# Rebuilding the first step of a fused recurrence and feed-forward kernel: order of the loads, scalings and transposes

## The chip, the core and the metric

The kernel runs on one core of one Trainium2 chip. The metric is the device time of one execution in microseconds; lower is better. Three runs of the kernel before gave 597.99, 598.65 and 599.09 us, median 598.65.

## The reference

Two blocks in a row, in float32. The first is a recurrence over time, for 4 batches and 8 heads of 48 channels, 768 tokens each; the second is a feed-forward block on the 3072 tokens.

```python
for t in range(S):
    kt, vt, rt, wt = (k[:, :, t], v[:, :, t], r[:, :, t], w[:, :, t])
    cur = np.einsum('bhd,bhe->bhde', u[None] * kt, vt)
    y[:, :, t] = np.einsum('bhd,bhde->bhe', rt, state + cur)
    state = wt[:, :, :, None] * state + np.einsum('bhd,bhe->bhde', kt, vt)
...
x = y.transpose(0, 2, 1, 3).reshape(B * S, H * D)      # 3072 x 384
h = x @ w_in                                           # 384 x 2048
g = h * erf(softplus(h))
out = g @ w_out                                        # 2048 x 384
```

The two weight matrices are given in double precision and are turned into float32 on the chip, from pairs of 32-bit words.

## The kernel before, in words

**Steps.** The work is cut into 12 steps. A step takes one chunk of 128 tokens of two of the four batches, with all heads: 16 pairs of batch and head. Steps alternate between the two pairs of batches; steps 0 and 1 have no state before them. In the document "step one" or "the first step" is `s == 0`, "step two" is `s == 1`.

**Recurrence.** Inside a step the decays are handled by a ladder of six levels (`attend`, L625). At level n blocks of 2^(n-1) tokens are joined. `level_products` (L444) issues 64 small matmuls, the products of R with K. `scale` (L257, the instruction is L263) then multiplies half of R and half of K, in place in the tile `in`, by the products of decays of their blocks, which `prepare` (L267) made on GpSimd (L315, tile `tot_sb`). `take_level` (L460) copies what belongs to this level from PSUM into `own`, with a mask on VectorE (L464) up to level five and by ScalarE copies (L471) at level six. Level one uses a copy `rk1` of R and K with the bonus u multiplied into half of it: in the first step VectorE does that for R (L284, L288) and ScalarE for K (L292, L295), for one batch at a time. The matmuls of a level wait for the scaling of the level before, and the scaling waits until the matmuls have read their operands.

**After the ladder.** `from_own` (L477, matmul L486) adds what is inside the chunk to `y` in PSUM, for one half of the heads at a time. K is transposed by TensorE (L680) and copied to `kT` by ScalarE (L684). `state_part` (L531, matmul L538) makes the change of the state for both halves of the chunk. The state after the first half goes to `middle` (L712), is faded on GpSimd (L713) and added to the second part for the next state (L715). `through_state` (L500) adds the state's share to `y` (L512), copies `y` to `y3` and `xT` (L519 to L522), and sends six small transfers (L526) that fill up the rows of `xT` from `y3`: three from SP's queue, three from ScalarE's.

**Feed-forward.** `hidden` (L744) multiplies `w_in_sb` with `xT` (L777) and copies to `h` (L786), in eight pieces per step; `project` and `project_fast` multiply with `w_out_sb`. The feed-forward of a step runs between the levels of the steps after it: `beside` (L925) issues a piece behind each level, so the first pieces (L777) come in step two and need `xT` of step one and the weight pairs one after another.

**Weights.** `convert` (L185) is a generator that is sent letters. Each pair of weight rows is loaded ("l", L199), scaled on ScalarE ("s": the high words into a PSUM tile `pp1`, L212, the low words to `rest`, L214), shifted on VectorE ("h", L220), joined with its sign on VectorE (L228) and with the low part on GpSimd (L232; "o"). "j" stands for "ho". The table `CONVERT` says which letters are sent at which place of which of the first four steps; place n stands behind level n+1.

**Order.** All instructions of an engine run in the order in which the program issues them; SP's queue of transfers too. Transfers use eight semaphores in turn, so a transfer also waits until the one eight before it has landed. PSUM has two tiles of two banks for products (`pp0`, `pp1`), two banks for `m` and two for `y`. `keep_busy` (L635), `stay_warm` (L643) and the 20 matmuls at L1026 compute nothing that is used; they keep TensorE busy.

Of the kernel before, what the change touches and what calls it, by code (L numbers as in the profile page):

```python
# [61 lines left out]
def kernel(  # L62
# [81 lines left out]
    def load_w(s, parts=1):  # L144
        ws[s] = ins.tile([P, JP, C], FP32, name="w")
        n = JP // parts
        for i in range(parts):
            nc.sync.dma_start(
                out=ws[s][:, i * n : (i + 1) * n], in_=rkw[s][:, 2, i * n : (i + 1) * n]
            )  # L150

    def load_step(s, parts=1):
        t = ins.tile([P, 2, JP, C], FP32, name="in")
        vt = ins.tile([P, NH, D], FP32, name="v")
        n = JP // parts
        for i in range(parts):
            nc.sync.dma_start(
                out=t[:, :, i * n : (i + 1) * n], in_=rkw[s][:, 0:2, i * n : (i + 1) * n]
            )
        if s <= DIRECT:  # L160
            load_w(s, parts)
        if not s:
            nc.sync.dma_start(out=mask_sb[:], in_=masks)
        elif s == 2:
            nc.sync.dma_start(out=block_sb[:], in_=block_mask)
            nc.sync.dma_start(out=u_row[:], in_=u_rows)
# [18 lines left out]
    def convert(weights):  # L185
# [5 lines left out]
        def load(i):  # L191
# [3 lines left out]
            if src.dtype == FP32:  # L195
# [3 lines left out]
            nc.sync.dma_start(  # L199
                out=words[:].rearrange("p i n two -> p i (n two)"), in_=src.bitcast(I32)  # L200
            )
            held[i] = [words]

        def scale(i):
            if i in held:
                words = held[i][0]
                low, high = words[:, :, :, 0], words[:, :, :, 1]
                base = ps_p.tile([P, 2, NP * C], FP32, name="pp1")[:, :, :DM]
                rest = wide.tile([P, 2, DM], I32, name="rest", bufs=2)


                nc.scalar.mul(out=base, in_=high.bitcast(FP32), mul=2.0**-112)  # L212

                nc.scalar.mul(out=rest[:], in_=low.bitcast(U32), mul=2.0**-29)  # L214
                held[i] += [base.bitcast(I32), rest]

        def shift(i):
            if i in held:
                bits = held[i][1]
                nc.vector.tensor_scalar(  # L220
                    out=bits, in0=bits, scalar1=3, scalar2=None, op0=ALU.logical_shift_left
                )

        def join(i):
            if i in held:
                words, bits, rest = held.pop(i)
                into = weights[i][0].bitcast(I32)
                nc.vector.scalar_tensor_tensor(  # L228
                    out=into, in0=words[:, :, :, 1], scalar=-(1 << 31), in1=bits,
                    op0=ALU.bitwise_and, op1=ALU.bitwise_or,  # L230
                )
                nc.gpsimd.tensor_tensor(out=into, in0=into, in1=rest[:], op=ALU.add)  # L232

        stages = {"l": load, "s": scale, "h": shift, "o": join}
        done = dict.fromkeys(stages, 0)
        for _ in range(3):
            load(done["l"])
            done["l"] += 1
        while True:
            what = yield  # L240
            for stage in {"j": "ho"}.get(what, what):
                stages[stage](done[stage])
                done[stage] += 1
            if weights[0][1].dtype != FP32:
                turns["converting"] = 0 < done["s"] and done["o"] < len(weights)
                turns["next"] = 0
# [10 lines left out]
    def scale(s, level):  # L257

        in_t, tots = loaded[s][0], ready[s][1]
        half, nb = 1 << (level - 1), JP * C >> level  # L260
        n = 1 if s > DIRECT and level == LOG else 2
# [238 lines left out]
    def through_state(s, xT):  # L500
# [19 lines left out]
        for j in range(NJ):  # L520
            nc.scalar.copy(xT[:, 0:2, j * C : (j + 1) * C], y[:, 0, j])
        nc.scalar.copy(xT[:, 2, :].rearrange("p (j t) -> p j t", j=NJ), y[:, 1, :, 0])  # L522
        for kk in range(KT):
            n = D // KT
            for e, queue in enumerate((nc.sync, nc.sync if s > DIRECT else nc.scalar)):
# [5 lines left out]
    def state_part(s, kT, ps):  # L531

        vt = loaded[s][1]
        for n in range(JP):
            for h in range(1 if s >= n_steps - SPC else NC):
                for e in range(NE):
                    t = slice(h * HC, (h + 1) * HC)
                    nc.tensor.matmul(  # L538
                        ps[h][rows(e), n, :D],
# [32 lines left out]
    def attend_late(s, run):  # L572
# [38 lines left out]
        ps = [ps[:, h] for h in range(NC)]  # L611
# [587 lines left out]
```

## Time and profile before

| | us |
|---|---|
| median of three runs | 598.65 |
| the profiled execution | 598.5 |
| its span | 596.3 |
| TensorE busy in the span | 584.7 |
| VectorE, ScalarE, GpSimd busy | 440.1, 361.8, 274.5 |
| first matmul of the feed-forward (L777) starts at | 34.40 |
| TensorE busy from 75 to 596 | 517.3 of 521 |
| DMA traffic in the span | 63.33 MB, of it 18.05 MB in the first 80 us |

Times of instructions count from the start of the span. A row of the timeline has the start, the busy time, the engine, the line of the kernel, the operation, the tile written and the tiles read, the shapes, how many were merged, and in brackets how long the engine was idle before it and what ended that. PE is TensorE, DVE VectorE, ACT ScalarE, POOL GpSimd, SP the engine whose queue issues most transfers; a name with a q is the engine's own queue. A float32 matmul appears as two passes, each with a load of weights (PEld) and a matmul.

### The profile page before, as it was taken

To read this page: it belongs to the slowest core of one execution; us is meant where nothing else is said; L and a number is where in the kernel's file an instruction comes from. 1 tells how busy PE (TensorE), PEld (TensorE's weight loads), DVE (VectorE), ACT (ScalarE), POOL (GpSimd) and SP (SyncE) were. 2 spreads that over 40 slices of the span, in tenths; PEclk is the share of its full clock that TensorE was granted. 3 is DMA by queue.
4 is the path that set the end of the run, shared out by engine and by line. 5 is a ranking of instruction groups with operands and counts; after the bars stand their busy time and mean duration, and the time that the engine had idled before them with its cause. 6 is when DMAs were issued, how large, how long until landed. Compare 5 with 4: busy or idle time off the path is not lost.

```text
span 596.3 us, 16645 instructions
## 1 busy us (share of the span) xinstructions
PE 584.7 (98%) x7290; PEld 501.7 (84%) x7290; DVE 440.1 (74%) x516; ACT 361.8 (61%) x473; POOL 274.5 (46%) x296
## 2 busy tenths in 40 slices
PE   8889999999999999999999999999999999999997
PEld 7667788678758758898898898898898898898997
DVE  5688598799996799799799799799799525023140
ACT  2547788717534398765765666666666664746710
POOL 4348365610588549749449449449459000000000
PEclk9999999999999999999999999999999999999999
DMA  8377381541315324334334335334331300000000
GB/s 320 124 278 234 118 290 58 217 141 20 134 38 159 66 95 168 71 108 169 72 107 168 73 106 169 73 107 134 71 107 54 71 9 26 2 21 13 2 27 26
DMA packets 51376, 63.33 MB, mean 106 GB/s; under 512 B 34920, under 2 KB 40296, under 8 KB 49896
## 3 DMA queue, kind: packets, MB, share of 16 engines
q1 hardware_dynamic: 50824, 62.03, 32.3%
q8 instruction: 57, 0.93, 0.6%
q10 hardware_dynamic: 480, 0.25, 0.2%
q14 instruction: 15, 0.12, 0.1%
HBM read 52.39 MB, written 8.69 MB: 102 GB/s over the span
## 4 chain that ended last, share of the span: by engine, by line
PE 88%; DVE 6%; issue 2%; ACT 2%; DMA 1%; POOL 1%; SPq 0%; DVEq 0%; ACTq 0%; POOLq 0%
PE m L777 40%; PE m L885 28%; PE m L809 8%; PE pp L452 6%; PE y L486 2%; DVE in L263 2%; PE pp L538 1%; PE y L512 1%; DMA in<-in_rkw 1%; PE pp L680 1%; DVE sums L367 1%; DVE words L381 1%; DVE own L464 1%; ACT rk L292 1%; DVE w_in_sb L228 0%
## 5 line engine op out<-in xcount | busy, mean ns | idle before, releaser
L777 PE MATMUL m<-xT,w_in_sb 128*128 128x256 f32 x1152 | 257.3, 382 | 2.3 <-DVE w_in_sb L228 1.3
L777 PEld LDWEIGHTS m<-xT,w_in_sb 128*128 128x128 f32 x1152 | 216.0, 190 | 34.5 <-issue 3.7
L786 ACT COPY h<-m 128x512 f32<-128x512 f32 x96 | 55.6, 580 | 84.2 <-PE m L777 84.1
L263 DVE TENSOR_TENSOR in<-in,tot_sb 128x1024 f32<-128x1024 f32 (+1 forms) x60 | 78.3, 1305 | 24.9 <-PE pp L452 23.8
L377 POOL TENSOR_TENSOR rk<-words 128x528 f32<-128x528 f32 (+3 forms) x28 | 41.6, 1485 | 91.4 <-DVE sums L367 81.0
L381 POOL TENSOR_TENSOR words<-words,rest 128x528 f32<-128x528 f32 (+10 forms) x77 | 79.1, 1027 | 6.0
L809 PE MATMUL m<-w_out_sb,h 128*128 128x384 f32 x192 | 64.3, 491 | 0.0
L809 PEld LDWEIGHTS m<-w_out_sb,h 128*128 128x128 f32 x192 | 35.7, 190 | 23.6
L885 PE MATMUL m<-mixed,h 128*128 128x192 f32 x288 | 51.1, 331 | 0.0
L885 PE MATMUL m<-w_out_sb,h 128*128 128x192 f32 x288 | 50.3, 329 | 0.0
L733 ACT ACT_TABLE_LOAD x36 | 46.2, 1283 | 2.4 <-issue 1.7
L885 PEld LDWEIGHTS m<-w_out_sb,h 128*128 128x128 f32 x288 | 46.9, 190 | 0.5
L885 PEld LDWEIGHTS m<-mixed,h 128*128 128x128 f32 x288 | 46.6, 190 | 0.9
L737 ACT ACT_TABLE_LOAD x36 | 46.2, 1283 | 1.7 <-DVE room L868 1.1
L452 PEld LDWEIGHTS pp<-in 48*64 48x64 f32 (+1 forms) x2368 | 34.0, 125 | 14.8 <-issue 8.1
L885 PE MATMUL m<-w_out_sb,room 128*128 128x192 f32 x256 | 44.2, 326 | 0.0
L452 PE MATMUL pp<-in 48*64 48x64 f32 (+1 forms) x2368 | 38.7, 212 | 4.0 <-issue 1.8
L315 POOL TENSOR_TENSOR tot_sb<-tot_sb 128x256 f32<-128x256 f32 (+4 forms) x60 | 40.4, 674 | 4.5
L885 PEld LDWEIGHTS m<-w_out_sb,room 128*128 128x128 f32 x256 | 42.0, 190 | 0.0
L742 DVE TENSOR_TENSOR h<-h,y 128x1024 f32<-128x1024 f32 x17 | 20.7, 1215 | 28.3 <-ACT y L737 28.2
L733 ACT ACTIVATE room<-h 128x1024 f32<-128x1024 f32 x36 | 38.1, 1057 | 0.4
L742 DVE TENSOR_TENSOR h<-h,pp 128x1024 f32<-128x1024 f32 x19 | 23.1, 1213 | 19.3 <-ACT pp L737 19.2
(123 smaller groups left out, 826.3 us busy)
## 6 DMA issues: line engine op xcount, KB each, us to landing
in<-in_rkw SPq DMA_DIRECT2D x11, 1024.0 KB, 5.1
words<-in_moe_w_in SPq DMA_DIRECT2D x8, 768.0 KB, 5.5
words<-in_moe_w_out SPq DMA_DIRECT2D x8, 768.0 KB, 4.6
words<-in_rk_rows SPq DMA_DIRECT2D x8, 768.0 KB, 6.2
w<-in_rkw SPq DMA_DIRECT2D x11, 512.0 KB, 7.0
v<-in_v SPq DMA_DIRECT2D x12, 384.0 KB, 6.0
out<-o SPq DMA_DIRECT2D x24, 192.0 KB, 2.4
rest<-in_w_rows SPq DMA_DIRECT2D x8, 384.0 KB, 5.0
```

The lines of the kernel that those rows point to most:

```text
L263: nc.vector.tensor_mul(halves, halves, view(tots[level - 1], 0, [[1, n], [2, nb], [0, half]]))
L315: nc.gpsimd.tensor_mul(new, pair[:, :, 0], pair[:, :, 1])
L377: engine.tensor_mul(terms[n], r[:, :, n:], k[:, :, : near - n])
L381: engine.tensor_mul(k[:, :, :m], k[:, :, :m], w[:, :, n : n + m])
L452: nc.tensor.matmul(pp[s0 : s0 + m, e, n, :m], lhsT=rk[rows(e), 1, n, s0 : s0 + m], rhs=rk[rows(e), 0, n, t0 : t0 + m], start=True, stop=True,)
L733: nc.scalar.activation(sp_room, chunks[0], AF.Softplus)
L737: nc.scalar.activation(at, sp_room, AF.Erf)
L742: nc.vector.tensor_mul(h, h, at)
L777: nc.tensor.matmul(ps[:, ff, :], lhsT=w_in_sb[:, g * FG + f + ff, kk * P : (kk + 1) * P], rhs=xT[:, kk, :], start=kk == 0, stop=kk == KT - 1,)
L786: nc.scalar.copy(h[:, f : f + FT, :], ps[:])
L809: nc.tensor.matmul(ps[j][:], lhsT=gs[g][:, f, j * C : (j + 1) * C], rhs=w_out_sb[:, g * FG + f, :], start=g + f == 0, stop=g == NG - 1 and ...
L885: nc.tensor.matmul(to, lhsT=a[:, f], rhs=b[:, f], start=start and f == 0, stop=f == FG - 1, skip_group_check=True,)
```

## The change

In the first step (`s == 0`) and around it:

- The loads of the first step are cut by columns and reordered (`load_first`): both R and K of the first batch, u, R of the second batch, w of the first batch, K of the second, w of the second, masks, v. Before, u came first, then R and K of the first batch, R and K of the second, and w.
- The input of steps one to three and the weight words are loaded by two transfers each (`load_halves`). One weight pair is loaded ahead of step two's input, two behind it; before, three were ahead of it.
- Level one's scaling is done batch by batch, and level six's for K first, then for R. keep_busy is left out at level six. The conversion of the first mask moves from VectorE to ScalarE.
- The transposes of K come ahead of the first half of y, and a fence (a small VectorE read of y, also used in the later steps) behind it. Only the first half of the state's matmuls stands ahead of `through_state`; the second half and the sum for the next state stand behind it. The copy to `middle` is split between ScalarE and VectorE. The stay_warm matmuls of the first step go.
- `xT` is copied part by part, and of its six transfers SP issues four and ScalarE two.
- Scaling of a weight pair is split into the high words ("b") and the low words ("r"). The first two pairs use two `m` tiles in place of `pp1`; the first is scaled at level one, the second between the fading and `through_state`. While `turns["converting"]` is not set, products alternate between `pp0` and `pp1`; it is now set from the third pair on.
- The warming matmuls at the start are 8 of 256 columns in place of 20 of 128.

The core of the diff:

```diff
+    def load_halves(dst, src):
+        for i in range(2):
+            nc.sync.dma_start(out=dst[:, i], in_=src[:, i])
...
+    def load_first():
...
+        n = JP // NJ
+        b0, b1 = slice(0, n), slice(n, JP)
+        nc.sync.dma_start(out=t[:, :, b0], in_=rkw[0][:, 0:2, b0])
+        nc.sync.dma_start(out=u_sb[:], in_=u)
+        nc.sync.dma_start(out=t[:, 0, b1], in_=rkw[0][:, 0, b1])
+        nc.sync.dma_start(out=ws[0][:, b0], in_=rkw[0][:, 2, b0])
+        nc.sync.dma_start(out=t[:, 1, b1], in_=rkw[0][:, 1, b1])
+        nc.sync.dma_start(out=ws[0][:, b1], in_=rkw[0][:, 2, b1])
+        nc.sync.dma_start(out=mask_sb[:], in_=masks)
+        nc.sync.dma_start(out=vt[:], in_=v[0])
...
+        if s < DIRECT:
+            load_halves(t, rkw[s])
...
+        def scale_high(i):
+            if i in held:
+                high = held[i][0][:, :, :, 1].bitcast(FP32)
+                if i < 2:
+                    base = [ps_m.tile([P, NP * C], FP32, name="m")[:, :DM] for _ in range(2)]
+                    parts = [(base[n], high[:, n], n) for n in range(2)]
...
+                for to, of, _ in parts:
+                    nc.scalar.mul(out=to, in_=of, mul=2.0**-112)
...
-            for stage in {"j": "ho"}.get(what, what):
+            for stage in {"j": "ho", "s": "br"}.get(what, what):
...
-                turns["converting"] = 0 < done["s"] and done["o"] < len(weights)
+            if weights[0][1].dtype != FP32 and done["b"] > 2:
+                turns["converting"] = done["o"] < len(weights)
...
+        if not s:
+            for kk, q in enumerate((y[:, 0, :, 0], y[:, 0, :, 1], y[:, 1, :, 0])):
+                nc.scalar.copy(by_kk[kk], q)
...
+        by_scalar = {(1, 1), (2, 0)} if not s else {(kk, 1) for kk in range(KT) if s <= DIRECT}
...
+        if not s:
+            nc.scalar.copy(first[:], mask_sb[:, 0, :])
...
+            if not s and level == 1:
+                for j in range(NJ):
+                    scale(s, level, batch=j)
+            elif not s and level == LOG:
+                for only in (1, 0):
+                    scale(s, level, only=only)
+            else:
+                scale(s, level)
+            if level < LOG:
+                keep_busy(DM, DM // 2)
...
-        from_own(s, own, 1)
+        if s:
+            from_own(s, own, 1)
...
         if not s:
-            stay_warm()
+            from_own(s, own, 1)
+            fence()
...
+        state_part(s, kT, ps, (0,) if not s else range(NC))
         from_own(s, own, 0)
         if not s:
-            stay_warm(1, products([P, NP * C]))
+            nc.scalar.copy(middle[rows(1)], ps[0][1][rows(1), :, :D])
+            nc.vector.tensor_copy(middle[rows(0)], ps[0][0][rows(0), :, :D])
+            fade()
+            conversion.send("b")
+            through_state(s, xT)
+            place(LOG + 1)
+            second = products([P, NE, JP, HC], 1)
+            ps.append([second[:, e] for e in range(NE)])
+            state_part(s, kT, ps, (1,))
+            to_next()
...
     CONVERT = (
-        ("", "", "", "", "", "s", "jls", "j", "sl"),
+        ("s", "", "", "", "", "j", "r", "jl", "sl"),
...
-        for _ in range(20):
-            nc.tensor.matmul(warm[:], lhsT=ident[:], rhs=ident[:], start=True, stop=True)
+        for _ in range(8):
+            nc.tensor.matmul(
+                warm[:], lhsT=ident[:], rhs=ident[:, None, :].to_broadcast([P, NC, P]),
+                start=True, stop=True,
+            )
```

## Prediction

> **What bounds the kernel now.** I read the page first, then the chain of waits by time, then the first 36 us instruction by instruction, then the DMA and instruction-fetch records of that stretch.
>
> From the page, the busy shares and the chain:
>
> ```profile
> PE 584.7 (98%) x7290; PEld 501.7 (84%) x7290; DVE 440.1 (74%) x516; ACT 361.8 (61%) x473; POOL 274.5 (46%) x296
> ...
> PE 88%; DVE 6%; issue 2%; ACT 2%; DMA 1%; POOL 1%; SPq 0%; DVEq 0%; ACTq 0%; POOLq 0%
> ```
>
> TensorE sets the time nearly everywhere. The change rebuilds the first of the twelve steps, so the question is when the dense matmuls (L777) begin. Until then they have no input; afterwards the matmuls follow one another, and whatever starts them earlier moves the end by as much. The timeline of the first 36 us:
>
> ```profile
> 6.68 1.08 ACT L292 ACTIVATE rk<-in,u_sb 128x64 f32<-128x64 f32 x4 [4.46 <-DMA in<-in_rkw]
> ...
> 10.06 1.24 PE L638 MATMUL y<-s,ident 128*128 128x384 f32 x4
> ...
> 15.45 0.56 PE L452 MATMUL pp<-in 48*64 48x64 f32 x18 [0.72 <-issue]
> ...
> 21.37 0.67 PE L452 MATMUL pp<-in 48*64 48x64 f32 x26 [0.62 <-issue]
> ...
> 23.42 0.76 PE L452 MATMUL pp<-in 48*32 48x32 f32 x64 [0.21 <-DVE in L263]
> ...
> 24.28 1.22 DVE L263 TENSOR_TENSOR in<-in,tot_sb 128x1024 f32<-128x1024 f32 x1 [0.28 <-PE pp L452]
> ...
> 26.33 0.97 DVE L220 TENSOR_SCALAR pp<-pp 128x768 int32<-128x768 int32 x1 [0.83 <-ACT pp L212]
> ...
> 27.27 0.80 ACT L684 COPY kT<-pp 128x768 f32<-128x768 f32 x1
> ...
> 29.09 1.14 DVE L712 COPY middle<-m 48x384 f32<-48x384 f32 x2 [0.80 <-PE m L538]
> ...
> 30.49 0.67 PE L512 MATMUL y<-in,middle 48*48 48x64 f32 x32
> ...
> 31.22 0.37 ACT L519 COPY y<-y 128x256 f32<-128x256 f32 x1 [1.17 <-PE y L512]
> ...
> 32.17 1.86 SPq L526 DMA_DIRECT2D xT<-y  x3
> ...
> 34.40 1.76 PE L777 MATMUL m<-xT,w_in_sb 128*128 128x256 f32 x5 [1.26 <-DVE w_in_sb L228]
> ```
>
> ScalarE's first multiply waits for the second input transfer (6.56 us), though its data came with the first (5.19). Levels two to six are a ladder: matmuls, then VectorE's scaling, then the next matmuls. Twice TensorE stops inside a burst with "issue" (0.72 and 0.62 us). L1 to L6 end at 24.2; the state, y, the copies and six small transfers take until 34.4, and the third part of xT until 35.68.
>
> The two stops are instruction fetches. Counting TensorE's instruction records, they lie exactly 256 instructions apart, and a third (0.48 us, at 51.70) five times 256 further. The instruction queue has one packet shortly before each; this is the window 12.9 to 13.2 us:
>
> ```profile
> q1 hardware_dynamic: 21, 0.12, 94.6%
> q8 instruction: 1, 0.02, 23.1%
> ```
>
> The packets begin at 13.03 and 19.01, 3.2 and 3.6 us after TensorE entered the block before; with the DMA engines idle (21.37 to 22.51, 26.0 to 26.95) it is only about 1.1. From packet to running again takes 2.4 us each time. So a block costs 5.6 to 5.9 us under load, about 3.5 without.
>
> [...] the loads then have 8 rows per engine, of 6 KB (0.235 us each, 1.9 in sum) or 8 KB (0.31 each, 2.5), and the fetch waited 2.1 and 2.4 us beyond the idle 1.1. [...] here L232 takes 1.83 or 2.67 us. [...] Here the warming matmuls go from 213 to 111 ns at 6.68 us.
>
> **The change part by part.**
>
> *Loads by columns.* The first input is issued at 0.74 instead of 1.19 (u goes second), so the same bytes land 0.45 sooner: 4.75. R and K of the second batch are now apart, so ScalarE starts on K of batch one at 4.9, hidden. The last input of level one is K of batch two, with 1.31 MB up to it, which landed at 7.71: now 7.26 (bounds 6.8 to 7.4). ScalarE: four multiplies 0.25 apart, the copy 0.42, ending 8.7. Matmuls of batch two 0.63, the keep_busy matmuls 1.17 (10.06 to 11.23): level two starts at 10.5 instead of 11.23.
>
> *Scaling by batches.* Two VectorE halves of about 0.65 for one of 1.23. The first runs at 6.4 beside the waiting; the second ends at 9.4, before keep_busy does. Cost nothing; without that cover, 0.2. The mask's conversion (0.60 on VectorE) moves to ScalarE, idle there after 8.7: nothing on the path.
>
> *Levels two to five.* A level is 2.56 us (17.38 to 19.95). Starts: 10.5, 13.05, 15.6, 18.2. Now the fetch. Eight warming matmuls for twenty are 48 instructions fewer, so the block ends move to the tenth matmul of level two (10.7), the start of level four and the third-last matmul of level five. Pieces of 3 and 4 KB rows (half of 0.235 and 0.31: 1.0 and 1.3 us per packet) let the fetch in sooner: 10.7 + 1.1 + 1.3 + 2.4 = 15.5, just in time; then 15.65 + 1.1 + 1.0 + 2.4 = 20.15 against 19.3. Level five ends at 20.3, not 22.04. Bounds: the old 5.7 per block gives 22.2; no stop at all gives 19.4. Level six starts 1.35 later (22.04 to 23.42): 21.65, a gain of 1.8.
>
> *Level six to y.* K's scaling starts 0.86 in, at 22.5, and takes 0.69; R's ends at 23.85. VectorE then has the shift and join of the first weight pair, moved ahead and in halves: four of about 0.55, to 26.05. The new fence (16 elements, no row; at least 0.1, at most the 0.53 of the mask's copy; I take 0.2) ends at 26.25. Behind it on VectorE stands half of the copy to middle (0.57, other half on ScalarE): 26.85. On TensorE the second half of y waits for the fence, 0.63 to 26.9. Beside this: transposes 23.2 to 24.2, first half of y, kT 0.80 to 25.05, one half of the state's matmuls to 25.7, all earlier. through_state starts at 27.0: 5.35 after level six instead of 7.07. Gain now 3.5.
>
> *Moved behind y.* The second half of the state's matmuls (0.47), fade (0.84, behind a join of 1.83 to 2.67 on GpSimd) and the additions to the next state run beside the transfers of xT; if they are late, level one's scaling of step two is: due 34.3, expected 31.8. The second pair's scaling (two ScalarE halves, 0.9) ends at 27.4, 0.3 ahead of the copies of y. stay_warm (1.02 and 1.13) goes, off the path now.
>
> *xT.* ScalarE copies by part, so the first transfer leaves 0.69 after the copies begin instead of 0.95; but SP carries four of the six, each about 0.62 to issue: the last leaves at 2.6 instead of 2.55 and lands near 1.95 later. That loses 0.2. Dense matmuls: first 31.1, third part of xT 32.4 instead of 35.68. Gain 3.3.
>
> *Queues.* Step two's input passes two weight pairs on SP and lands near 14 instead of 17.9; it is needed by ScalarE only then. Weight pair four (words 3) goes the other way: from SP at 28.36 to behind the xT transfers, near 31. Halving adds 0.33 us of SP issue per load, free while SP waits (16.65 us at a stretch).
>
> *Step two.* Sixty-four fewer TensorE instructions move the block ends; the stop at 51.70 falls into a stretch with 8 us per block and should go: 0.4. Sum: 3.3 + 0.4 = 3.7.
>
> The profiled run took 598.5, its span 596.3 and 2.2 around it; the median of the three runs is 598.65. 598.65 - 3.7 = 594.95, say 595.0.
>
> **Rivals.** (A) The above, 595.0; own range 593.8 to 596.2. (B) The fetch is as slow as now: level five ends at 22.2 whatever the loads do, the gain of 1.8 there becomes -0.1, and the total 596.9; with step two's stop also back, 597.3. For it: two stops already. Against: half-size packets. (C) No stop at all: 0.9 better, 594.0. For it: the fetch is late by 0.9 only. (D) The clock falls because the warming matmuls are gone: one window of 3.4 us at half speed in the dense part costs 1.7: 596.7. Against: no idle stretch above 0.9 us between 21.6 and 31. (E) Slower: weight pair four lands late. Its scaling in step two is due near 37.6; issued at 31 to 31.6, at the weights' median of 5.5 us it lands at 37.1. Beyond 37.6 each us delays the pieces by one, and past 41.3 the gain is gone. At the 12.1 us that the step inputs needed behind other loads it lands at 43.7: 6.1 lost, 601.0. Against: nothing large is queued ahead of it.
>
> **How the numbers follow.** Chances: A 0.52, B 0.20, C 0.17, D 0.05, E 0.06. This kernel's runs can tell 0.2% (1.2 us) from no change, so faster means under 597.45: A, C, D and 0.12 of B make 0.86; the rest of B, with a miss in the loads on top, 0.08 within; slower is E, 0.06. Range 593.6 (C with the loads 0.4 earlier) to 597.3 (B's slow end): outside it lie E and some 0.10 of the tails.
>
> **What will show it.** Right: first ScalarE multiply near 4.9; level two at 10.5; TensorE's "issue" stops under 1 us in levels four and five; level six near 21.6; middle to y near 27; L777 at 31 and no "issue" stop in level five of step two. Wrong: level six at 23.4 or later (fetch as before), L777 rows waiting for w_in_sb in step two (E), or L777 of 400 ns and more spacing (D).

## The result and the profile after

The changed kernel is slower: median 600.73 us (598.84 to 604.12) against 598.41 for the kernel before (22 runs of each), ratio 1.0040 with a 95% interval of 1.0026 to 1.0054. Forecast were 595.0 us, with a range of 593.6 to 597.3 and a chance of 0.06 for slower. The profiled execution of the changed kernel took 598.84, the least of its 22; its span is 597.1.

The page of the changed kernel, busy shares and chain:

```profile
PE 581.7 (97%) x7258; PEld 499.1 (84%) x7258; DVE 440.7 (74%) x521; ACT 362.6 (61%) x477; POOL 271.7 (46%) x296
...
PE 84%; DVE 6%; ACT 5%; issue 3%; DMA 2%; ACTq 0%; SPq 0%; POOL 0%; DVEq 0%; POOLq 0%
```

TensorE is busy 3.0 us less, mostly by warming matmuls that went, yet the span is 0.8 longer; on the chain "issue" and DMA have each gained a point. Where, the timeline says (lines of the changed kernel: L331 is the old L292, L491 the old L452, L302 the old L263, L534 the fence, L551 through_state, L558 and L562 the copies of y, L572 the small transfers, L856 the old L777):

```profile
5.16 1.08 ACT L331 ACTIVATE rk<-in,u_sb 128x64 f32<-128x64 f32 x4 [2.93 <-DMA u_sb<-in_u]
...
7.89 1.08 ACT L331 ACTIVATE rk<-in,u_sb 128x64 f32<-128x64 f32 x4 [1.33 <-DMA in<-in_rkw]
...
11.12 1.16 PE L491 MATMUL pp<-in 48*64 48x64 f32 x64
...
19.02 1.15 PE L491 MATMUL pp<-in 48*64 48x64 f32 x61 [0.33 <-DVE in L302]
21.74 0.33 PE L491 MATMUL pp<-in 48*64 48x64 f32 x3 [1.57 <-issue]
...
23.44 0.76 PE L491 MATMUL pp<-in 48*32 48x32 f32 x64 [0.20 <-DVE in L302]
...
27.36 0.17 DVE L534 COPY seen<-y 128x16 f32<-128x16 f32 x1
...
28.67 0.66 PE L551 MATMUL y<-in,middle 48*48 48x64 f32 x32 [0.28 <-DVE middle L775]
...
29.43 0.37 ACT L558 COPY y<-y 128x256 f32<-128x256 f32 x1
...
30.10 2.88 SPq L572 DMA_DIRECT2D xT<-y  x4
...
34.12 2.18 PE L856 MATMUL m<-xT,w_in_sb 128*128 128x256 f32 x9 [1.64 <-DMA xT<-y]
```

Read from the top: level two begins at 11.12 (before 11.23). Level three runs without its old stop, so level five begins at 19.02 (before 19.95). Level six begins at 23.44 (before 23.42): all of the lead is lost in one "issue" of 1.57 us, three matmuls before the end of level five. From there to through_state the change does what it was costed at: 28.67 instead of 30.49. Then the first dense matmul waits 1.64 us for xT and comes at 34.12, only 0.28 before the old 34.40. And one step further, in level four of step two, TensorE stops again:

```profile
45.48 0.80 PE L491 MATMUL pp<-in 48*64 48x64 f32 x38
47.57 0.68 PE L491 MATMUL pp<-in 48*64 48x64 f32 x26 [1.28 <-issue]
48.17 1.13 PE L856 MATMUL m<-xT,w_in_sb 128*128 128x256 f32 x4
```

The third dense piece, at 42.69, was still 0.73 ahead of the kernel before (43.42); the fourth, at 48.17, is 0.87 behind (47.30). By the tenth the two are level (73.52 and 73.49).

They stay level for long: TensorE is 0.06 behind at 204 us. At 253 it is 0.77 behind, and so it ends. In between lies a later step, in which ScalarE sends three of the small transfers and then loads a table for its next work. First the kernel before, then the changed one:

```profile
204.44 1.95 ACTq L526 DMA_DIRECT2D xT<-y  x3
...
206.43 1.28 ACT L733 ACT_TABLE_LOAD   x1 [1.73 <-issue]
```

```profile
204.50 2.57 ACTq L572 DMA_DIRECT2D xT<-y  x3
...
207.11 1.28 ACT L812 ACT_TABLE_LOAD   x1 [2.36 <-issue]
...
230.42 4.80 PE L856 MATMUL m<-xT,w_in_sb 128*128 128x256 f32 x21 [0.38 <-ACT o L897]
```

The issue takes 0.62 us longer, ScalarE stays that far behind, and at 230 us TensorE waits for one of its copies (L897).

So the profile shows why nothing was won and where 0.8 us were lost, but not the 2.3 of the medians. For that every execution's **granted clock** is needed. The profiles of warm20, late_whole and lww_33 (below) have a mean of 0.997, and up to 58 us each has one stretch of 3.41 us with a granted clock of 0.50; 3.41 / 2 / 597 = 0.0029. By these numbers a mean of 0.997 is estimated to be one such stretch. Below 0.999 were 17 of 22 executions of the changed kernel, and 41 of 202 of the kernel before in the four later comparisons. Executions at 0.999 or more have the median 599.22 (before 598.2 to 598.3), those below it 601.42.

### The profile page after: what moved, and what is told of

The parts are those of the page before. It is cut to its first block, busy times and chain, and to the rows that moved or that the text cites. A ratio compares the mean times of both kernels' runs of the same rounds, so it can differ in the third digit from the quotient of the medians.

```text
span 597.1 us, 16616 instructions
## 1 busy us (share of the span) xinstructions
PE 581.7 (97%) x7258; PEld 499.1 (84%) x7258; DVE 440.7 (74%) x521; ACT 362.6 (61%) x477; POOL 271.7 (46%) x296
## 4 chain that ended last, share of the span: by engine, by line
PE 84%; DVE 6%; ACT 5%; issue 3%; DMA 2%; ACTq 0%; SPq 0%; POOL 0%; DVEq 0%; POOLq 0%
PE m L856 39%; PE m L964 28%; PE pp L491 5%; PE m L888 4%; PE y L525 2%; PE pp L586 1%; PE y L551 1%; DVE in L302 1%; DMA xT<-y 1%; PE pp L737 1%; DMA in<-in_rkw 1%; DVE own L503 1%; ACT room L812 1%; DVE sums L406 1%; ACT L816 1%
## 5 line engine op out<-in xcount | busy, mean ns | idle before, releaser
L856 PE MATMUL m<-xT,w_in_sb 128*128 128x256 f32 x1152 | 257.3, 382 | 2.9 <-DMA xT<-y 2.5
L856 PEld LDWEIGHTS m<-xT,w_in_sb 128*128 128x128 f32 x1152 | 216.0, 190 | 35.0 <-issue 3.6
L302 DVE TENSOR_TENSOR in<-in,tot_sb 128x1024 f32<-128x1024 f32 (+1 forms) x59 | 77.9, 1321 | 26.7 <-PE pp L491 25.6
L491 PEld LDWEIGHTS pp<-in 48*64 48x64 f32 (+1 forms) x2368 | 33.9, 126 | 15.8 <-issue 9.5
L491 PE MATMUL pp<-in 48*64 48x64 f32 (+1 forms) x2368 | 38.5, 212 | 5.2 <-issue 2.9
L821 DVE TENSOR_TENSOR h<-h,pp 128x1024 f32<-128x1024 f32 x19 | 23.1, 1213 | 19.9 <-ACT pp L816 19.9
```

Source lines behind the costliest of these rows:

```text
L302: nc.vector.tensor_mul(halves, halves, view(tots[level - 1], 0, [[1, n], [2, nb], [0, half]]))
L491: nc.tensor.matmul(pp[s0 : s0 + m, e, n, :m], lhsT=rk[rows(e), 1, n, s0 : s0 + m], rhs=rk[rows(e), 0, n, t0 : t0 + m], start=True, stop=True,)
L821: nc.vector.tensor_mul(h, h, at)
L856: nc.tensor.matmul(ps[:, ff, :], lhsT=w_in_sb[:, g * FG + f + ff, kk * P : (kk + 1) * P], rhs=xT[:, kk, :], start=kk == 0, stop=kk == KT - 1,)
```

## The experiments

Theory F in the expectations: the time is lost in stops while TensorE waits for its next 256 instructions, and each long stop costs a second time because the clock drops after it. Its rivals are named in each expectation. "Stop" is an "issue" wait of TensorE in a burst; "packet" is a 16 KB packet of the instruction queue; "entry" is TensorE's start on a new block of 256 instructions (in the changed kernel's trace the records after its two stops, at 21.74 and 47.57, lie 1024 TensorE instructions apart, four times 256). Theory C is the granted clock in the runs on the clock, and the meeting of a packet with the transfers of xT in the runs on these. "Clock low: 15 of 22" counts executions with a mean clock below 0.999. Ratios are to the kernel before in the same comparison.

### Where the stops come from

**repeat**: the changed kernel, unchanged.

> The changed kernel once more, unedited. Its executions spread from 598.8 to 604.1 us where those of the kernel before spread from 597.5 to 600.3, and the profiled one was the fastest of them. Theory F (TensorE's instruction fetch: its packets wait behind loads on a DMA engine, and small transfers wait behind them): the time lost against the first profile lies in TensorE's 'issue' stops and in transfers of which one of the sixteen parts lands late; a slower execution shows longer such stops in steps one to four and the same matmul durations. Theory W (weights late): rows of L856 that wait for w_in_sb or of ScalarE that wait for words. Median again about 600.7.

600.75 us, ratio 1.0033 (1.0020 to 1.0045), clock low in 15 of 22. Its profile has the stop in level five (1.40 us) but not the one of step two. The loss is repeatable; the second stop comes and goes. Theory F expected the same matmul durations in slow executions; granted clocks down to 0.986 speak against that.

**late_words**: the second and third weight pairs are loaded only after level four; a small copy and transfer make SP wait for it.

```diff
+            if not s and level == 4:
+                gate = const.tile([P, 16], FP32, name="gate")
+                nc.vector.tensor_copy(out=gate[:], in_=own[:, 0, :16])
+                scratch = dram.tile([P, 16], FP32, name="scratch")
+                nc.sync.dma_start(out=scratch[:], in_=gate[:])
+                for _ in range(2):
+                    conversion.send("l")
...
-        for _ in range(2):
-            conversion.send("l")
```

> Weight pairs two and three are asked for only when level four of the first step is taken (a small copy and a transfer to memory hold SP back), so that few loads are under way when TensorE asks for the block of instructions that it needs near the end of level five. Theory F: the fetch packet, at 19.27 before, comes near 17.6; the stop of 1.57 us in level five goes to 0 to 0.3, level six starts near 22.0 in place of 23.44, and 1.2 to 1.5 us come off the changed kernel's time unless a later stop takes them. Theory N (a fixed time of some 5.5 us per block whatever the loads do): the stop stays 1.5 us and level six stays at 23.4.

598.16 us, ratio 0.9992 (0.9983 to 1.0001): 2.6 less than repeat in the same comparison, where 1.2 to 1.5 was expected. The timeline of levels five and six:

```profile
19.13 1.16 PE L491 MATMUL pp<-in 48*64 48x64 f32 x64 [0.72 <-DVE in L302]
...
21.71 0.76 PE L491 MATMUL pp<-in 48*32 48x32 f32 x64 [0.25 <-DVE in L302]
```

All 64 matmuls of level five are in one row and level six is 1.73 sooner. The packet came 1.13 us after TensorE entered the block at 16.1, instead of 2.90. So the stop of level five, 1.57 us with the weights loading there and none without them, goes with the wait of the fetch. The clock is still low in 12 of 22, but here these executions are no slower than the rest (medians 598.14 and 598.16).

**warm20**: the 20 old warming matmuls in place of the 8, 48 instructions more, so that the block ends lie where they lay before.

> The eight warming matmuls are replaced by the twenty of the kernel before: 48 more TensorE instructions, so every block of 256 ends 48 instructions earlier in the work. Theory F: the stops move: a small one (0 to 0.5 us) in the middle of level three, one of about 0.5 to 1 us in the middle of level five, so level six starts 0.3 to 0.8 earlier than 23.44; the stop of 1.28 us in step two moves as well. A theory in which the stops belong to what is computed there (a wait that the profile does not show) leaves them at the last three matmuls of level five.

598.73 us, ratio 1.0002 (0.9988 to 1.0016), clock low in 8 of 13. The stop moves to level three (1.17 us, at 16.17), level five has none; level six at 23.80. The place of the stop follows the instruction count, as theory F had it; the sizes were not as expected (level six at 22.6 to 23.1). That the time is 2 us below the changed kernel is not explained by these stops alone: the stop of step two and the loss behind 204 us are also absent from this profile.

**whole**: the halves are undone.

```diff
-        for i in range(2):
-            nc.sync.dma_start(out=dst[:, i], in_=src[:, i])
+        nc.sync.dma_start(out=dst, in_=src)
...
-            load_halves(t, rkw[s])
+            load_halves(t[:], rkw[s][:, 0:2])
```

> load_halves is undone: step inputs and weight words come in one transfer each, as before. Theory F: the rows double to 6 and 8 KB, so each fetch packet waits 0.5 to 1 us longer under load: level five's stop grows from 1.57 to about 2.2, level six starts near 24.0, and the time rises by 0.5 to 1. A theory in which the number of transfers costs (semaphores in turn, issue on SP): the time falls by 0.5 to 2 us.

599.52 us, ratio 1.0017 (1.0006 to 1.0029), clock low in 15 of 22. Better, not worse: theory F's expectation fell, and the other one, that the number of transfers costs 0.5 to 2 us, gave the right size (1.2). The semaphores in turn can be seen in the kernel before: SP's eleventh, twelfth and thirteenth transfers wait 0.8, 0.8 and 0.3 us and are issued at 6.58, 7.72 and 8.39, when the third, fourth and fifth have landed (6.56, 7.71 and 8.37). The packets came 2.54 and 2.21 us after the two block entries; with halves 2.66 and 2.90. Halving the transfers did not shorten this wait at all.

### The clock

**cold_before**: the kernel before without keep_busy at level six and without the two stay_warm matmuls of the first step.

> The kernel before, without three things that the change also takes away: keep_busy at level six of the first step and its two stay_warm matmuls. Nothing else is edited. Theory C (the granted TensorE clock drops to half for one or two stretches of 3.4 us where TensorE has too little to do, and the removed matmuls were what kept it up): the share of executions with a granted clock under 0.999 rises from 13 of 67 to more than half, and the median rises by 1 to 2.5 us although the kernel does less. Theory F alone (instruction fetch): clock and time stay, within 0.5 us.

598.77 us, ratio 1.0010 (0.9999 to 1.0022), clock low in 7 of 14, against 8 of 41 of the kernel before. More than half and 1 to 2.5 us were expected; half came, and the 0.4 us are not clear of noise.

**warm**: the changed kernel with two pieces of warming put back, one matmul at level six and a second one while TensorE waits for xT.

```diff
-            if level < LOG:
-                keep_busy(DM, DM // 2)
+            keep_busy(*((DM, DM // 2) if level < LOG else (DM,)))
...
-                stay_warm()
+                stay_warm(2)
```

> The changed kernel with keep_busy put back at level six (384 columns, in the wait for K's scaling) and with two stay_warm matmuls in place of one while step two waits for xT. Theory C: executions with a clock under 0.999 fall from 32 of 44 to fewer than 15 of 44, and the median from 600.7 to 598.9, which is what the changed kernel takes at full clock. Theory F alone: no change, or up to 0.5 us slower for the added work.

599.68 us, ratio 1.0018 (1.0003 to 1.0033), clock low in 10 of 19. Expected were 598.9 and under a third of low clocks; neither came. The stops remain, and the profile shows what they do. Windows of this profile (width, busy time of each engine with its count, granted clock, DMA share, GB/s):

```profile
core 0: us, PE busy (x) PEld busy (x) DVE busy (x) ACT busy (x) POOL busy (x), PEclk, DMA share, GB/s
19.20:22.61 3.41, 1.53 (x65) 1.28 (x58) 0.53 (x2) 0.00 (x0) 1.36 (x5) 1.00 0.13 46
22.61:26.02 3.41, 3.41 (x70) 2.11 (x68) 2.29 (x4) 0.67 (x2) 0.00 (x0) 0.50 0.02 5
46.50:49.91 3.41, 1.85 (x68) 1.32 (x66) 1.78 (x2) 0.44 (x1) 2.46 (x2) 1.00 1.06 366
49.91:53.33 3.42, 3.42 (x8) 2.73 (x9) 3.33 (x4) 3.35 (x8) 2.95 (x3) 0.50 0.63 235
```

The first window holds the stop of level five, the third that of step two; TensorE is busy 1.53 and 1.85 of 3.41 us, and the window after each runs at half the clock (0.50).

**late_warm**, late words and this warming together, and **late_warm_whole**, these and whole transfers:

> The same two edits on the kernel whose weight pairs two and three load after level four. If C and F are both at work and independent: 598.16 less the 0.9 to 1.5 us that half clock cost its profiled execution (stay_warm 2.07 in place of 1.13 us, the first piece 3.45 in place of 2.8): 596.5 to 597.3, clock near 1. If the clock plays no part: 598.2 or more.

> As before, and load_halves undone. The changed kernel gained 1.2 us (600.73 to 599.52) when load_halves was undone, against theory F's expectation of a loss. If that gain is of the transfers themselves, 0.5 to 1.2 us come off late_warm here too. If it came from where the fetch packets of steps one and two happened to fall, the two kernels lie within 0.4 us.

late_warm: 598.69 us, ratio 1.0001 (0.9989 to 1.0013), clock low in 6 of 14; 596.5 to 597.3 was expected; its profile has a stop of 1.52 us in step two. late_warm_whole: **596.60 us, ratio 0.9971 (0.9960 to 0.9982)**, clock low in 0 of 6. It beats both kernels. The two differ by 2.1 us, more than either expectation had (0.5 to 1.2, or under 0.4), and only in whole or halved transfers. Its timeline:

```profile
21.64 0.76 PE L490 MATMUL pp<-in 48*32 48x32 f32 x64 [0.25 <-DVE in L301]
...
26.88 0.66 PE L550 MATMUL y<-in,middle 48*48 48x64 f32 x32 [0.28 <-DVE middle L780]
...
30.01 1.98 PE L693 MATMUL m<-w,ident 128*128 128x512 f32 x4
32.81 2.40 PE L861 MATMUL m<-xT,w_in_sb 128*128 128x256 f32 x10 [0.81 <-DMA xT<-y]
```

Level six at 21.64 and through_state at 26.88 are the prediction's 21.65 and 27.0. That they agree is luck in part: not smaller pieces freed the fetch (2.66 and 2.90 us from entry to packet in the changed kernel, 2.54 and 2.21 in whole), but loads moved out of its way (1.13 in late_words).

**late_whole**, the same without the warming, and **tail_only**, with only the second matmul during the wait for xT:

> The changed kernel with words two and three loaded only after level four, and with the big loads as whole transfers instead of halves; none of the removed warmers is put back. Theory F (stops of instruction fetch cost the time, and drop the clock with them): without stops the granted clock is 0.999 or more in nearly all executions, and the time is 596.6 to 597.0 us, as with the warmers put back. Rival W (the warmers that the change removed held the clock): the clock is below 0.999 in half of the executions, mostly 0.997, and the time is 597.5 to 598.2 us, as with the late words alone (598.16).

> Late words and whole transfers with one of the two removed pieces of warming put back: the second warmer of level one of step two, which TensorE runs while it waits for xT; the dummy product at level six stays out. If the wait for xT is where the clock is lost (the profile without either piece had the half clock right after it, from 34.09), the granted clock is 0.999 or more in over three quarters of the executions and the median is 596.2 to 596.9. If it is the gap at level six, nearly half of the executions stay below 0.999 as without either piece (9 of 14), and the median is 597.5 to 598.5.

late_whole: 598.33 us, ratio 0.9988 (0.9973 to 1.0004), clock low in 9 of 14, as rival W had it. The 5 executions at full clock took 596.02 to 596.60; late_words, with halves, has a median of 598.16 at full clock. tail_only: 597.51, ratio 0.9980 (0.9966 to 0.9994), clock low in 3 of 14, so at full clock in 11 of 14, as expected of the wait for xT; the median is 0.6 above the expected range, and its profile has a stop of 1.58 us in step two. The stretch around the wait for xT, in late_whole first, then in late_warm_whole:

```profile
30.68:34.09 3.41, 1.33 (x4) 0.51 (x4) 3.35 (x4) 1.71 (x2) 1.07 (x1) 1.00 0.19 36
34.09:37.50 3.41, 3.41 (x10) 2.70 (x9) 0.87 (x1) 0.00 (x0) 0.00 (x0) 0.50 0.92 317
```

```profile
30.68:34.09 3.41, 2.60 (x10) 1.43 (x9) 3.38 (x3) 1.33 (x2) 0.40 (x1) 1.00 0.33 58
34.09:37.50 3.41, 3.41 (x76) 2.80 (x75) 0.90 (x2) 0.59 (x1) 0.00 (x0) 1.00 1.01 401
```

In late_whole TensorE is busy 1.33 us of the window and the first dense pieces run at half speed (granted clock 0.50): 10 matmuls in 3.41 us. With one more warming matmul here (and one at level six) it is 2.60 and full speed. These are late_whole's windows; cut along its own, late_warm_whole is nowhere below 2.60 either.

### The transfers of xT

**lww_33**: late_warm_whole with the six transfers split three and three.

```diff
-        by_scalar = {(1, 1), (2, 0)} if not s else {(kk, 1) for kk in range(KT) if s <= DIRECT}
+        by_scalar = {(kk, 1) for kk in range(KT) if s <= DIRECT}
```

> The best version so far (596.6 us) with the six small transfers of xT split three and three over the two queues as in the kernel before, instead of four and two. The prediction put the split at 0.2 us. If it is the split, the first matmul on xT starts 0.2 to 0.6 us sooner than 32.81 and the time is 596.1 to 596.4; if the fetched packet on one DMA engine sets the landing, it stays within 0.2 us of 32.81 and the time at 596.6.

596.43 us (22 runs), ratio 0.9973 (0.9962 to 0.9985), first L861 at 32.87. The split costs nothing that can be seen.

**lww_pad**: late_warm_whole with 32 warming matmuls of 64 columns in place of 8 of 256.

> The best version so far (late words, whole transfers, warmers put back; 596.6 us), with 32 warmers of 64 columns in the place of 8 of 256 ahead of it, so that the end of a block of 256 TensorE instructions is crossed 96 instructions sooner and the next block is fetched before the six small transfers of xT instead of among them. Theory F: the packet no longer delays the sixteenth part of these transfers; the first matmul on xT starts at 31.6 to 31.9 us instead of 32.81, and the time is 595.6 to 596.0 us. Rival (the small transfers are late for another reason, the issue on their queues): the first matmul stays at 32.5 to 32.9, and the time at 596.6. It can also lose: if another block's end falls into level three or five, a stop of 0.5 to 1.5 us is seen there and the time is 597 us.

606.26 us (5 runs), ratio 1.0140 (1.0116 to 1.0163). The design was bad: the 64 passes came 0.213 us apart and ran to 15.5 instead of 8.1, and the full clock came only at 20.61 (four passes of 384 columns took 2.29 us at 17.44; they take 1.24 in the kernel before, at 10.06). The packet did move, to 38.18, beside the first transfer of xT at 38.11, and the first matmul came 2.83 us after that transfer instead of 4.49. The landing followed the packet, as theory F had it; the time says nothing.

**lww_fill** and **after_fill**: 24 small dummy products (96 instructions) at level six, while TensorE waits, in late_warm_whole and in the changed kernel; nothing earlier is touched.

```diff
+        def fill(n):
+            zeros = states[1][0][:].rearrange("p n d -> p (n d)")
+            for k in range(n if not s else 0):
+                e, s0 = k % NE, (k // NE) % 2 * HC
+                nc.tensor.matmul(
+                    y[:].rearrange("p e j q t -> p (e j q t)")[s0 : s0 + HC, (1 - e) * 512 : (1 - e) * 512 + HC],
+                    lhsT=ident[rows(e), s0 : s0 + HC], rhs=zeros[rows(e), :HC],
+                    start=True, stop=True, skip_group_check=True,
+                )
```

> The best version (late words, whole transfers, warmers put back; 596.6 us) with 24 small dummy products (96 TensorE instructions on tiles of 48 x 64) at level six, while TensorE waits for the multiply of K; the fetch that lay among the six small transfers of xT is asked for 96 instructions sooner, and none of the work ahead of level six is touched. Theory C (the landing collides with the fetched packet): the packet comes at 28.0 to 28.4 us, about with the first small transfer, the first matmul on xT starts 2.3 to 2.9 us after the first issue instead of 4.5, at 31.2 to 31.8 instead of 32.81, and the time is 595.2 to 596.0. Rival (the transfers land late for a reason of their own, the number on each queue or the 400-byte rows): 4.0 us or more after the first issue, and 596.4 or more.

> The changed kernel with the same 24 dummy products at level six and nothing else. The stop in level five stays (1.6 us). Theory C: the packet comes at 29.5 to 30.2 us instead of 31.73, the first matmul on xT starts 2.3 to 3.0 us after the first small transfer is issued (4.02 in the changed kernel), so near 33.0 instead of 34.12, and 0.7 to 1.2 us of the 2.3 that the changed kernel lost come back: 599.4 to 600.0. Rival: 4.0 us after the first issue as now, and 600.4 or more.

after_fill: 598.80 us, ratio 1.0002 (0.9987 to 1.0017): 1.9 us better than the changed kernel by dummy work alone, more than the 0.7 to 1.2 expected. Not all of it is xT: its profile also has a shorter stop in level five (0.77 us) and lacks the 0.7 us lost behind 204 us. Clock low in 7 of 14. The issues of xT with their time to landing, from 29 to 34 us in the changed kernel, then 29 to 33 us in after_fill, and the first dense matmul of the latter:

```profile
xT<-y SPq DMA_DIRECT2D x4, 16.0 KB, 3.0
```

```profile
xT<-y SPq DMA_DIRECT2D x4, 16.0 KB, 1.8
```

```profile
29.82 2.52 SPq L572 DMA_DIRECT2D xT<-y  x4
...
32.43 3.20 PE L868 MATMUL m<-xT,w_in_sb 128*128 128x256 f32 x12 [0.66 <-DMA xT<-y]
```

The landing fell from 3.0 to 1.8 us. lww_fill: first matmul 2.99 us after the first transfer (4.49 before), as theory C says; but 596.88 us (ratio 0.9979, 0.9969 to 0.9989) is no better than late_warm_whole. The filling took 0.8 us at level six and a new stop of 0.58 fell into through_state: the first transfer left at 30.29 instead of 28.32, and the first dense matmul came at 33.28 instead of 32.81. That part of the expectation fell.

All the profiles with these six transfers sort by when the packet came, counted from the first transfer's issue:

| packet after the first transfer, us | first dense matmul after it, us | profiles |
|---|---|---|
| -0.17 to 0.17 | 2.23 to 2.99 | before, cold_before, before_late, after_fill, lww_pad, lww_fill |
| 0.79 to 1.38 | 3.77 to 4.30 | warm20, late_words, lww_33 |
| 1.62 to 1.99 | 3.99 to 4.66 | after, repeat, whole, warm, late_warm, late_warm_whole, late_whole |
| 2.25 | 3.62 | tail_only |

In before and lww_33 the wait of the first dense matmul is put down to the weights, not to xT.

The loss behind 204 us sorts in the same way. Where the packet began 0.02 to 0.40 ahead of the transfers there, ScalarE's three issues took 1.81 to 2.02 us and TensorE lost at most 0.07 (before, cold_before, before_late, warm20, lww_fill, after_fill). Where it began 0.11 to 0.75 behind the first of them, they took 2.38 to 2.76 and TensorE lost 0.71 to 0.81 (nine profiles). Between them lie lww_33 (packet 0.16 behind; 2.16; lost 0.22) and lww_pad (packet 0.20 ahead; 2.27; lost 0.32). No run was made to test this.

### The kernel before, with late words

**before_late**: in the kernel before, only the loads of weight pairs two and three are moved behind level four.

> The kernel before, changed in one thing: words two and three are loaded only after level four. Theory F: the stop in level five of the kernel before (0.6 to 0.8 us) is gone, level six comes 0.5 to 0.9 us sooner, and the time is 597.5 to 597.9 us against 598.4. Rival (the stop is covered by the wait for K and R, which bound level six anyway): level six at 23.4 as before, and the time the same within 0.1%.

599.04 us, ratio 1.0002 (0.9991 to 1.0012), clock low in 9 of 22. In its profile the stop in level five is gone, level six comes at 22.95 (before 23.42) and the first dense matmul at 34.18 (before 34.40). Theory F's 0.5 to 0.9 did not come in the median. The rival's "level six as before" is wrong too; its "same time" is what was measured. Yet the profiled execution has a span 0.9 shorter (595.4 against 596.3); why the median shows none of it is open.

## Why the prediction was wrong, by its own steps

**Now the fetch: wrong, and the step that failed.** "Pieces of 3 and 4 KB rows let the fetch in sooner ... Level five ends at 20.3." It ended at 22.07. Of the difference 0.7 is a later entry into the second block (16.4, not 15.65), and 0.8 is the wait until its packet: 2.90 us, where 1.1 + 1.0 was put. That the fetch waits for 8 rows of another queue was the author's estimate, from two numbers of one profile, and no run shows it: the changed rows do take half the time (0.12 us for 3 KB), and the wait did not follow. Removing the load from that stretch shortens it to 1.13 (late_words), halving its pieces does not (2.90 with halves, 2.21 in whole). Rival B was this case in kind, but it was priced at 596.9, with all behind level five as forecast.

**Loads by columns: right in kind, mis-sized.** The first multiply started at 5.16 (4.9), as u landed only at 5.06, and the second part of K landed at 7.86 (7.26). Level two: 11.12, not 10.5. The gain of 0.73 was 0.11.

**Level six to y: right.** 5.23 us against 5.35; the fence took 0.17 (0.2).

**xT: wrong.** From the copy of y to the first dense matmul it took 4.69 us, not 3.4 (the 3.18 of the kernel before and 0.2). The term "SP carries four of the six ... loses 0.2" was not it (lww_33). Five of the six transfers had 15 of their 16 parts early, and the last part later: four of them by 1.2 to 1.5 us, the sixth by 0.4 (second transfer: 15 by 32.28, all at 33.78). A packet of instructions, 16 KB, had begun on one DMA engine at 31.73 and took 1.03. The earlier y brought the transfers under it; in the kernel before it began 0.17 ahead of them. after_fill moved the packet to 0.16 ahead of them, and the first dense matmul came 2.61 instead of 4.02 us after the first transfer: 1.4 back. Why the late part comes a microsecond after the packet's own end is not settled.

**Step two: wrong sign.** A stop of 0.48 was to vanish; one of 1.28 came. Its packet came 7.33 us after the entry into the block (45.16, entry at 37.8). Of all 17 profiles six show 6.9 to 7.6 us at this block and eleven 1.6 to 4.1: long and short ones with halves and with whole transfers, and both in the same kernel (after 7.33, repeat 3.40). What decides is open.

**Rival D: the cause that got too small a chance.** It had 0.05 and 1.7 us, against it "no idle stretch above 0.9 us". It was right in kind, judged by the wrong measure, and with one of two triggers: the clock is low more often with warming missing (cold_before, 7 of 14 against 8 of 41) and with TensorE's stops (warm, 10 of 19). No profile of the kernel before shows the 3.4 us at half speed that it reckoned with; those of the experiments do: the granted clock is 0.50 for 3.41 us in late_whole (from 34.09), warm20 (35.04) and lww_33 (47.38), twice in warm (22.61 and 49.91), and for two such windows in a row in late_words (28.22). The first full-speed stretch starts anywhere between 4.6 and 7.8 us in all profiles but lww_pad, while TensorE's work starts at 1.68 in each. The window ahead of a drop was not idle. Cut along each execution's own windows, sixteen profiles (all but lww_pad) have these cases from 10 us to nearly 60: TensorE busy 1.33, 1.53 or 1.68 us of 3.41, half clock (0.50) next in 3 of 3; 1.78 to 2.15, half clock next in 3 of 13; 2.16 or more, never, but for the second of the two half windows of late_words. In the kernel before, the lowest is 2.45. In the changed kernel the stop of level five is cut by a window's edge (2.28 and 2.25 on either side), and its profile keeps the clock; in warm it falls into one window (1.53) and the clock goes. So the same kernel has both kinds of executions, which fits the granted clocks; that the phase decides in each single run was not shown.

Each of the two triggers goes with low clocks by itself: with the stop of level five, but the warming put back, the clock is low in 10 of 19 (warm); without that stop, but without the warming too, in 9 of 14 (late_whole) and 12 of 22 (late_words); with both triggers in 32 of 44 (after and repeat). With neither it is low in 0 of 6 and 3 of 22 (late_warm_whole, lww_33), but in 6 of 14 in late_warm, whose transfers are halved and whose profile has the stop of step two.

**The halves: put down as free.** The prediction gave them 0.33 us of SP's issue per load, "free while SP waits". But once the words load late, whole transfers are worth 2 us even at full clock: 596.60 against 598.45 (late_warm_whole, late_warm), 596.13 against 598.16 (late_whole, late_words). The waits in the first step do not show it (1.06 and 1.11 us at the second block). In the first pair of profiles the difference is mostly the stop of step two (1.52 us), but profiles with whole transfers have that stop too (late_whole, tail_only, lww_33). What the halves cost is not shown.

**The sum.** 3.7 us were to be won. In the changed kernel's profile through_state is 1.8 ahead where 3.5 was forecast, for the loads and the fetch; the first dense matmul is 0.3 ahead, for xT; the tenth dense piece is level, for the stop of step two; and the end is 0.8 behind, for the later transfers. So "whatever starts them earlier moves the end by as much" was not safe either. At full clock the changed kernel is 0.4 (repeat) to 1.0 behind; the rest of the 2.3 us goes with the executions of low clock. That the clock alone makes it is not shown: these executions may have other stops too, and in late_words low clocks cost nothing.

What was there to be had is the 1.6 us of late_warm_whole (596.6 against 598.2 at full clock). It is 2.1 short of the sum: its first dense matmul is at 32.81 where 31.1 was worked out, and of the 2.5 us that its profile is ahead at 75 us, 0.7 is lost behind 204 us.

**Rival E** did not occur: no dense row of step two waited for its weights in the changed kernel's profile.

## What to carry to other kernels

A stretch of transfers that TensorE does not wait for can still stop it, through the instructions that it needs next (level five: 2.90 us from entry to packet with the weights loading, and a stop of 1.57; 1.13 and no stop without them, in late_words). Count 256 instructions at a time, note where the block ends fall, and keep heavy loads out of the microseconds behind each. When matmuls that compute nothing are removed, or a wait is shortened in one place and lengthened in another, add up TensorE's busy time in every window of 3.41 us at the worst phase (half the clock came next after 1.33 to 1.68 us in 3 of 3, after 1.78 to 2.15 in 3 of 13), and look at the granted clock of all executions, not at one profile. A gain in one place moves small transfers against everything else in the queues (those of xT, 16 KB each: 1.8 us to landing in after_fill, 3.0 in the changed kernel), in later steps too (issues of 2.57 us instead of 1.95 at 204 us): compare when both kernels reach the same matmuls all the way to the end, not only in the stage that was changed.

## What was not expected of the hardware

- A fetch of instructions mostly waited 0.3 to 1.6 us with little load and 2 to 7.6 with loads in flight (1.13 in late_words; 2.90 at level five and 7.33 at step two in the changed kernel), whether these were halved or not; from packet to running again it was 2.3 to 2.6 us (19.27 to 21.74 in the changed kernel).
- Where one packet of 16 KB on one of 16 DMA engines came among transfers of 16 KB, the last part of four of them landed 1.2 to 1.5 us after the others (after), and the issue of one took up to 1.92 us instead of 0.6 (lww_33).
- After a window in which TensorE is busy for 1.33 to 2.15 of 3.41 us the clock of the next one was 0.50 in 6 of 16 cases (late_whole, warm20, late_words, lww_33, and twice in warm).
- Warming by many narrow matmuls (64 columns, two loads of 128 x 128 weights each) did not bring the full clock in 13.8 us (lww_pad), though TensorE shows as busy throughout; with 256 columns it came 4 to 6 us after the first (5.64 in the changed kernel).
